# Tying the loads and the decoding of streamed weight tiles to places in the queues of a fused attention and MoE kernel

## The chip, the cores and the metric

The kernel runs on one core of a Trainium2 chip. The metric is the device time of one execution in microseconds (us); lower is better. Engines are called PE (TensorE), DVE (VectorE), ACT (ScalarE), POOL (GpSimd) and SP (SyncE, which issues DMAs here).

## What is computed

Attention with queries pooled in pairs, then two feed-forward layers. Inputs and weights are float64 on the host and reach the chip as pairs of 32-bit words.

```python
q_pool = q.reshape(B, H, S // 2, 2, D).mean(axis=3)          # B 2, H 8, S 1152, D 64
scores = np.matmul(q_pool, k.transpose(0, 1, 3, 2)) / np.sqrt(D)
attn = softmax(scores)                                        # max subtracted, 1e-9 in the sum
x = np.matmul(attn, v)                                        # -> [1152 tokens, 512]
h = x @ w_in                                                  # 512 -> 2048
g = (a0 + a1*h + a2*h**2 + a3*h**3) / (1 + |b0|*|h| + |b1|*h**2 + 1e-6)
x = g @ w_out                                                 # 2048 -> 512
h = x @ w2_in
g = np.maximum(h, 0) + np.log1p(np.exp(-np.abs(h)))
out = g @ w2_out
```

## The kernel before, in words

Every product is made from a high part and a low part of its operands (three matmuls for one). The attention works through NP = 8 pairs of heads. A pair has ST = 36 steps; step s makes one 128x288 block of scores (`s_step`, L436: two matmuls into a `pps` bank of PSUM, then the Exp on ACT, L449). Every second step `s_split` (L451) takes two blocks (tile `p`, 128x576): ACT casts them to the high part `ph` (L457) and POOL subtracts to get the low part `pl` (L121, a helper that all subtractions share). `pv` (L464, lines 471 to 473) multiplies both with V about seven steps later. While pair j runs its steps, the row maxima of pair j+1 are made (`p1_fill` on PE, L395; `p1_max` on DVE, L400), and its Q and K are turned and moved (`tr_k`, `tr_q`, `fcopy` DMAs at L209 on SP). There is no next pair during the last pair, so that DVE has little to do there.

The order is written out by hand: `at(t, fn)` collects functions with a step number on a common axis (pair j's steps are 36j to 36j+35), the list is sorted, and the functions run in that order. A tile scheduler then puts the instructions of every engine into a queue. It goes by that order but moves an instruction ahead of others as soon as its inputs and buffers are free in its own reckoning, and an engine works off its queue strictly in order. `behind(fn, engine)` keeps what `fn` issues on an engine behind a remembered instruction of that engine.

The 64 weight tiles (16 for each of four matrices) are streamed: `w_load` (L156) issues a 512 KB DMA on SP into one of two `wraw` buffers; `w_abs` (L171) makes the exponent right on ACT (L175) into one of three `pk` buffers; `w_conv` (L180) is two bit operations on DVE (L181 and L187; a third one, L184, only later); `w_split` (L191) casts the high part on ACT (L197) and subtracts the low part (L121, tile `w`) on POOL for the first NE = 3 tiles and on DVE for the rest. Together this is called decoding below. `pre` (L569) places the first 17 tiles in the attention: tiles 0 to 2 at steps 71, 107 and 143, and tiles 3 to 16 from step 242 on, one every four steps (load at t0, `w_abs` at t0+2, `w_conv` at t0+3 to t0+5, `w_split` at t0+7). The remaining tiles are decoded in the feed-forward part, paced by `w_step`. The tiles 3 to 16 live where the attention's buffers were: `close_early` at step 241, `close_even` at 262.

The first feed-forward layer works on 24 groups k of two column blocks: `up` (24 matmuls into a PSUM tile `h`, two buffers, L610), `act1_a` (three ACT passes over h), `act1_y` (three DVE passes; L636 is the last that reads h), `act1_b`, `act1_c`, and one group later `down1` (24 matmuls, `acc`, L660). The second layer does the same with a Softplus.

Of the kernel before, what the change touches and what calls it, by code (L numbers as in the profile page):

```python
# [21 lines left out]
    lv=0,  # L22
    pv=15,
    pvd=8,
    pq=8,
    tk=12,
    tkd=3,
# [21 lines left out]
    xb=19,  # L49
    w0=-1,  # L50
    wd=3,
    wc=25,
    wg=4,
    wh=1,
    ce=10,
# [30 lines left out]
def attn_moe_kernel(tc, q, k, v, w1_in, w1_out, moe_a, moe_b, w2_in, w2_out, out):  # L86
# [69 lines left out]
    def w_load(i):  # L156
        m, kind, f = order[i]
        src = (w1_in, w1_out, w2_in, w2_out)[2 * m + kind].bitcast(I32)
        raw = wst.tile([128, 512, 2], I32, tag="wraw", name="wraw", bufs=2)
        if kind == 0:  # L160
            nc.sync.dma_start(
                out=raw.rearrange("p (d f) e -> p d (f e)", d=ND),
                in_=src[:, f * 256:(f + 1) * 256].rearrange("(d p) f -> p d f", p=128),
            )
        else:
            nc.sync.dma_start(out=raw.rearrange("p f e -> p (f e)"), in_=src[f * 128:(f + 1) * 128, :])
        st["raw", i] = raw

    def w_abs(i):
        st["pk", i] = wst.tile([128, 512], I32, tag="pk", name="pk", bufs=3)  # L170
        o, hi = st["pk", i].bitcast(F32), st["raw", i][:, :, 1].bitcast(F32)  # L171
        if "second" in st:
            nc.scalar.activation(out=o, in_=hi, func=AF.Copy, scale=REBIAS)
        else:
            nc.scalar.activation(out=o, in_=hi, func=AF.Prelu, scale=REBIAS, alpha=SIGN)  # L175
            st["signed", i] = True
# [29 lines left out]
    QL = [[par[i].tile([74, 640], F32R, name=f"ql{i}{x}") for x in "ab"] for i in range(2)]  # L206
    V2 = [par[i].tile([128, 2, C, 192], F32R, name=f"v2{i}") for i in range(2)]
    def fcopy(out_, in_):
        nc.sync.dma_start(out=out_.bitcast(F32), in_=in_.bitcast(F32))  # L209

    def load_kq(j):
        b, h = j // NPB, 2 * (j % NPB)
# [225 lines left out]
    def s_step(j, s):  # L438
        g, c = divmod(s, C)
        x, half = divmod(g, 2)  # L440
        i = j % 2
        cs = qcols(x, half)
        ks = slice(c * 128, (c + 1) * 128)
        t = pps.tile([128, 512], F32, tag="s", name="s")[:, 0:HALF]
        nc.tensor.matmul(out=t, lhsT=KS[i][x][:, ks], rhs=QQ[i][x][:, cs], start=True, stop=False)  # L445
        nc.tensor.matmul(out=t, lhsT=KH[x][:, ks], rhs=QL[i][x][:, cs], start=False, stop=True)  # L446
        if s % 2 == 0:
            st["p"] = late.tile([128, 2, HALF], F32, tag="p", name="p", bufs=4)
        nc.scalar.activation(out=st["p"][:, s % 2], in_=t, func=AF.Exp)  # L449

    def s_split(j, s):  # L451
        p = st["pg", j, s]
        ph = late.tile([128, 2, HALF], F32R, tag="ph", name="ph", bufs=5)
        pl = late.tile([128, 2, HALF], F32R, tag="pl", name="pl", bufs=5)
        n = s // 2 + j * ST // 2
        if T["ph"] and n % T["ph"] == 0:
            nc.scalar.copy(out=ph, in_=p)  # L457
        else:
            nc.vector.tensor_copy(out=ph, in_=p)
        sub(nc.vector if T["lp"] and j == NP - 1 and n % T["lp"] == 0 else nc.gpsimd, pl, p, ph)  # L460
        for e in range(2):
            st["ph", j, s - 1 + e] = (ph[:, e], pl[:, e])
# [39 lines left out]
    for j in range(NP):  # L502
# [3 lines left out]
        for x in range(2):  # L506
            if j == 0:
                A(b1 + T["v0"] + T["pvd"] * x, lambda x=x: behind(lambda: prep_v(0, x), "act", "dve"), pr=7)
            else:
                if j == 1 and T["vb"]:  # L510
                    A(b1 + T["pv"] + T["pvd"] * x, lambda x=x: behind(lambda: prep_v(1, x), "act", "dves"), pr=7)
                else:
                    A(b1 + T["pv"] + T["pvd"] * x, prep_v, j, x, pr=7)
        if j == 0:
            A(b2 + 0, first_load)
            A(b2 + 1, warm, T["warm"])
# [49 lines left out]
            if g >= 2:  # L566
                A(b0 + C * g + T["xb"], xev_b, j, g, pr=3)

    def pre(i, t0, d, pool):  # L569
        at(t0, lambda: w_load(i))  # L570
        at(t0 + 2 * d, (lambda: behind(lambda: w_abs(i), "act")) if i < 2 else lambda: w_abs(i), 7)
        for n in range(3):
            at(t0 + 3 * d + d * n, lambda n=n: w_conv(i, n), 7)
        at(t0 + 7 * d, lambda: w_split(i, pool(), nc.vector if i >= NE else nc.gpsimd), 8)

    for i in range(NE):
        pre(i, ST * min(i + 2, NP - 2) + T["w0"] + 9 * max(0, i - NP + 4), T["wd"], lambda: we)

    def close_early():
        early.release()  # L580
# [7 lines left out]
    at(tc0, close_early)  # L588
    at(ST * (NP - 1) + T["ce"], close_even)
    for i in range(NRA + NRB):  # L590
        pre(NE + i, tc0 + 1 + T["wg"] * i, T["wh"], (lambda: st["wra"]) if i < NRA else (lambda: st["wrb"]))

    ph_ = pa_ = ap = wl_ = pt_ = pt2 = None

# [29 lines left out]

    def act1_a(h):
        m, s, p = T_("m", 2), T_("s", 2), T_("p", 2)
        nc.scalar.activation(out=m, in_=h, func=AF.Abs, scale=b_sb[:, 0:1])
        nc.scalar.activation(out=s, in_=h, func=AF.Square)
        nc.scalar.activation(out=p, in_=h, func=AF.Identity, scale=a_sb[:, 3:4], bias=a_sb[:, 2:3])
        return h, m, s, p  # L630

    def act1_y(h, m, s, p):
        V = nc.vector.scalar_tensor_tensor
        V(out=m, in0=s, scalar=b_sb[:, 1:2], in1=m, op0=ALU.mult, op1=ALU.add)
        nc.vector.tensor_mul(out=p, in0=h, in1=p)
        V(out=p, in0=p, scalar=a_sb[:, 1:2], in1=h, op0=ALU.add, op1=ALU.mult)  # L636
        return m, s, p

    def act1_b(m, r, p):
# [90 lines left out]
    if True:  # L730
# [66 lines left out]
        for k in range(NG + LAG1):  # L797
            if k == NG - 1:
                st["second"] = True
            if k < NG:  # L800
                for c, f in units[2 * k:2 * k + 2]:
# [2 lines left out]
                    h = up(0, c, f)  # L804
                    if c == (NCH - 1 if f < FH else 0):
                        freed.append(st["wp", (0, 0, f)])
                ga[k] = act1_a(h)
                ga[k] = act1_y(*ga[k])
            st["i"] = 2 * k
            w_pace()  # L810
            if 0 <= k - 1 < NG:
# [96 lines left out]
```

## Time and profile before

| | us |
|---|---|
| median of three runs | 764.52 (760.53, 764.52, 764.54) |
| the profiled execution | 760.95 |
| its span, first to last instruction | 759.2 |
| busy: PE / DVE / ACT / POOL | 725.5 / 540.8 / 493.7 / 295.0 |

The attention takes the first 338 us or so, the first layer goes to about 558 us, the second to the end. The page of the profile gives busy tenths in 40 slices of 19 us each. A busy PE is not a PE at its peak: matmuls overlap, so a stretch in which PE counts as busy throughout may still hold fewer matmuls than another.

### The profile page before, as it was taken

What the parts mean: (1) busy time and instruction counts of PE and PEld (TensorE: products, weight loads), DVE (VectorE), ACT (ScalarE), POOL (GpSimd) and SP (SyncE); (2) the same over time, 40 slices, a digit from 0 to 9 for tenths busy, and PEclk for the clock granted to TensorE, in tenths of its full rate; (3) what the DMA queues carried; (4) which work ended last, traced back from release to release, by engine and by line L of the source; (5) the groups of instructions that cost most, each with busy time, mean ns of one, the idle gap of its engine ahead of it and who ended that gap; (6) DMA issues with size and microseconds to landing.
All of it is one profiled execution on the core that took longest, in us unless ns stands there. A gap on an engine that the chain in (4) does not pass through costs nothing.

```text
span 759.2 us, 11696 instructions
## 1 busy us (share of the span) xinstructions
PE 725.5 (96%) x4273; PEld 680.3 (90%) x4273; DVE 540.8 (71%) x885; ACT 493.7 (65%) x921; POOL 295.0 (39%) x233
## 2 busy tenths in 40 slices
PE   8998999999999998887999999999999999999997
PEld 5698999999999997776999999999888789989986
DVE  5885877777777689389999999999997773111121
ACT  3377888888888888888777776876744553212120
POOL 5297888878787866960000000000243332000000
PEclk9999999999999999998999999999999999999999
DMA  6868664646454424023112221221234440001011
GB/s 184 203 155 177 166 163 103 138 105 149 100 119 101 93 64 130 30 83 111 56 57 60 80 84 56 83 60 52 84 111 139 137 141 0 1 1 42 0 42 43
DMA packets 60474, 70.32 MB, mean 93 GB/s; under 512 B 20008, under 2 KB 48512, under 8 KB 60416
## 3 DMA queue, kind: packets, MB, share of 16 engines
q1 hardware_dynamic: 59232, 68.58, 33.2%
q10 hardware_dynamic: 1184, 0.98, 0.4%
q8 instruction: 34, 0.56, 0.3%
q14 instruction: 24, 0.20, 0.1%
HBM read 47.71 MB, written 2.36 MB: 66 GB/s over the span
## 4 chain that ended last, share of the span: by engine, by line
PE 67%; DVE 17%; ACT 6%; DMA 6%; issue 3%; POOL 1%; SPq 0%; DVEq 0%; ACTq 0%; POOLq 0%
PE h L610 16%; PE p L395 10%; PE acc L702 9%; PE acc L660 8%; DMA wraw<-in_moe_w_in_dram 5%; PE s L445 4%; PE pv L473 4%; PE s L446 4%; PE pv L471 4%; PE pv L472 4%; DVE pk L187 3%; DVE pk L181 2%; DVE gl L121 2%; DVE w L121 1%; DVE pk L184 1%
## 5 line engine op out<-in xcount | busy, mean ns | idle before, releaser
L121 POOL TENSOR_TENSOR pl<-p,ph 128x576 fp32r<-128x576 f32 x144 | 208.6, 1465 | 60.4 <-ACT ph L457 33.8
L610 PE MATMUL h<-xh,w 128*128 128x384 f32 x768 | 198.6, 338 | 8.0 <-DVE p L636 8.0
L610 PEld LDWEIGHTS h<-xh,w 128*128 128x128 f32 x768 | 140.4, 190 | 11.0 <-issue 9.2
L400 DVE TENSOR_REDUCE nm<-p 128x1 f32<-128x384 f32 x216 | 116.5, 552 | 41.4 <-PE p L395 39.7
L121 POOL TENSOR_TENSOR w<-pk,w 128x512 fp32r<-128x512 f32 x26 | 41.5, 1598 | 250.0 <-ACT w L197 246.2
L449 ACT ACTIVATE p<-s 128x288 f32<-128x288 f32 x288 | 114.5, 408 | 25.4 <-PE s L446 23.2
L610 PE MATMUL h<-xl,w 128*128 128x384 f32 x384 | 129.7, 338 | 0.0
L121 DVE TENSOR_TENSOR gl<-p,gh 128x768 fp32r<-128x768 f32 (+1 forms) x49 | 48.4, 991 | 98.4 <-ACT gh L621 98.2
L457 ACT CAST ph<-p 128x576 fp32r<-128x576 f32 x144 | 96.9, 673 | 2.6
L660 PE MATMUL acc<-gh,w 128*128 128x384 f32 x384 | 92.7, 336 | 1.1 <-ACT gh L621 1.1
L473 PE MATMUL pv<-pl,v 128*128 128x288 f32 x288 | 87.0, 302 | 4.6 <-POOL pl L121 4.6
L702 PE MATMUL acc<-w,gh 128*128 128x512 f32 x288 | 90.3, 395 | 0.4 <-ACT gh L621 0.3
L471 PE MATMUL pv<-ph,v 128*128 128x288 f32 x288 | 86.2, 299 | 0.0
L472 PE MATMUL pv<-ph,v 128*64 128x288 f32 x288 | 85.1, 295 | 0.0
L690 ACT ACTIVATE p<-h 128x768 f32<-128x768 f32 (+1 forms) x25 | 19.5, 783 | 89.2 <-PE h L610 89.2
L610 PEld LDWEIGHTS h<-xl,w 128*128 128x128 f32 x384 | 72.7, 189 | 0.0
L660 PEld LDWEIGHTS acc<-gh,w 128*128 128x128 f32 x384 | 68.7, 188 | 2.1 <-ACT gh L621 2.1
L702 PEld LDWEIGHTS acc<-w,gh 128*128 128x128 f32 x288 | 53.5, 188 | 12.2 <-ACT gh L621 1.2
L473 PEld LDWEIGHTS pv<-pl,v 128*128 128x128 f32 x288 | 54.4, 189 | 8.3 <-POOL pl L121 7.0
L660 PE MATMUL acc<-gl,w 128*128 128x384 f32 x192 | 59.5, 338 | 1.0 <-DVE gl L121 1.0
L197 ACT CAST w<-pk 128x512 fp32r<-128x512 f32 x64 | 39.6, 619 | 31.8 <-DVE pk L187 31.8
L702 PE MATMUL acc<-w,gl 128*128 128x512 f32 x144 | 57.0, 396 | 1.1 <-DVE gl L121 1.1
(147 smaller groups left out, 1488.0 us busy)
## 6 DMA issues: line engine op xcount, KB each, us to landing
wraw<-in_moe_w_in_dram SPq DMA_DIRECT2D x32, 512.0 KB, 4.0
wraw<-in_moe_w_out_dram SPq DMA_DIRECT2D x32, 512.0 KB, 3.2
vr<-in_v_dram SPq DMA_DIRECT2D x8, 576.0 KB, 3.9
kr<-in_k_dram SPq DMA_DIRECT2D x15, 288.0 KB, 4.1
qr<-in_q_dram SPq DMA_DIRECT2D x15, 256.0 KB, 4.3
out_dram<-m SPq DMA_DIRECT2D x15, 128.0 KB, 1.8
kha<-ks0a SPq DMA_DIRECT2D x4, 288.0 KB, 3.1
khb<-ks0b SPq DMA_DIRECT2D x4, 288.0 KB, 4.3
```

Source lines behind the costliest of these rows:

```text
L121: return eng.tensor_tensor(out=o, in0=a, in1=b, op=ALU.subtract)
L197: nc.scalar.copy(out=w[:, 0], in_=g)
L395: m = nc.tensor.matmul(out=o, lhsT=l, rhs=r, start=(a == 0), stop=(a == len(mm) - 1))
L400: nc.vector.tensor_reduce(out=st["nm", j][:, t, e:e + 1], in_=st.pop(("p1", j, u)), axis=AX.X, op=ALU.max, negate=True)
L449: nc.scalar.activation(out=st["p"][:, s % 2], in_=t, func=AF.Exp)
L457: nc.scalar.copy(out=ph, in_=p)
L471: nc.tensor.matmul(out=st["pv", j, g], lhsT=h, rhs=ph, start=(c == 0), stop=False)
L472: nc.tensor.matmul(out=st["pv", j, g][0:64], lhsT=l, rhs=ph, start=False, stop=False)
L473: nc.tensor.matmul(out=st["pv", j, g], lhsT=h, rhs=pl, start=False, stop=(c == C - 1))
L610: nc.tensor.matmul(out=h, lhsT=w[:, wi, wd], rhs=x[:, d, xcols(c)], start=(n == 0), stop=(n == 3 * ND - 1))
L660: nc.tensor.matmul(out=st["acc", c, d], lhsT=w[:, wi, wd], rhs=g, start=(first and n == 0), stop=(last and n == 2))
L702: nc.tensor.matmul(out=st["acc", c, t], lhsT=g[:, t * 128:(t + 1) * 128], rhs=w[:, wi], start=(first and n == 0), stop=(last and n == 2))
```

## The change

- `pre` is rewritten: the load of a tile is placed at t0 and kept behind the last `fcopy` on SP, `w_abs` is placed at t0+5 and kept behind the last Exp on ACT, `w_conv` comes at t0+6 to t0+8, `w_split` at t0+10 and its ACT cast again behind the last Exp.
- Tiles 0 to 2 start at steps 72, 108 and 144. Tiles 3 to 16 start 11 steps earlier (`wc` 25 to 14: loads at steps 231, 235 and so on), which puts their `w_abs` 8 steps and their `w_split` 8 steps earlier; `close_early` moves with them to step 230, and the last pair's `prep_v` from steps 231 and 239 to 224 and 227.
- `wraw` gets three buffers, `pk` two.
- In the last pair every second cast to `ph` (nine of 18) is made by DVE.
- In the first layer `act1_a` makes `p` first, `act1_y` makes `m` last, and for the first two groups both are scheduled with high priority.

```diff
-    wc=25,
+    wc=14,
...
-        raw = wst.tile([128, 512, 2], I32, tag="wraw", name="wraw", bufs=2)
+        raw = wst.tile([128, 512, 2], I32, tag="wraw", name="wraw", bufs=3)
...
-        st["pk", i] = wst.tile([128, 512], I32, tag="pk", name="pk", bufs=3)
+        st["pk", i] = wst.tile([128, 512], I32, tag="pk", name="pk", bufs=2)
...
-        if T["ph"] and n % T["ph"] == 0:
+        if j == NP - 1 and n % 2:
+            nc.vector.tensor_copy(out=ph, in_=p)
+        else:
             nc.scalar.copy(out=ph, in_=p)
-        else:
-            nc.vector.tensor_copy(out=ph, in_=p)
...
-                    A(b1 + T["pv"] + T["pvd"] * x, prep_v, j, x, pr=7)
+                    A(b1 + (T["pv"] + T["pvd"] * x if j < NP - 1 else T["pe"] + T["ped"] * x), prep_v, j, x, pr=7)
...
-    def pre(i, t0, d, pool):
-        at(t0, lambda: w_load(i))
-        at(t0 + 2 * d, (lambda: behind(lambda: w_abs(i), "act")) if i < 2 else lambda: w_abs(i), 7)
+    def pre(i, t0, pool):
+        at(t0, lambda: behind(lambda: w_load(i), "sp"))
+        at(t0 + 5, lambda: behind(lambda: w_abs(i), "exp"), 7)
         for n in range(3):
-            at(t0 + 3 * d + d * n, lambda n=n: w_conv(i, n), 7)
-        at(t0 + 7 * d, lambda: w_split(i, pool(), nc.vector if i >= NE else nc.gpsimd), 8)
+            at(t0 + 6 + n, lambda n=n: w_conv(i, n), 7)
+        at(t0 + 10, lambda: behind(lambda: w_split(i, pool(), nc.vector if i >= NE else nc.gpsimd), "exp"), 8)
 
     for i in range(NE):
-        pre(i, ST * min(i + 2, NP - 2) + T["w0"] + 9 * max(0, i - NP + 4), T["wd"], lambda: we)
+        pre(i, ST * (i + 2), lambda: we)
...
     def act1_a(h):
         m, s, p = T_("m", 2), T_("s", 2), T_("p", 2)
+        nc.scalar.activation(out=p, in_=h, func=AF.Identity, scale=a_sb[:, 3:4], bias=a_sb[:, 2:3])
         nc.scalar.activation(out=m, in_=h, func=AF.Abs, scale=b_sb[:, 0:1])
         nc.scalar.activation(out=s, in_=h, func=AF.Square)
-        nc.scalar.activation(out=p, in_=h, func=AF.Identity, scale=a_sb[:, 3:4], bias=a_sb[:, 2:3])
...
-        V(out=m, in0=s, scalar=b_sb[:, 1:2], in1=m, op0=ALU.mult, op1=ALU.add)
         nc.vector.tensor_mul(out=p, in0=h, in1=p)
         V(out=p, in0=p, scalar=a_sb[:, 1:2], in1=h, op0=ALU.add, op1=ALU.mult)
+        V(out=m, in0=s, scalar=b_sb[:, 1:2], in1=m, op0=ALU.mult, op1=ALU.add)
...
-                ga[k] = act1_a(h)
-                ga[k] = act1_y(*ga[k])
+                with tc.high_priority() if k < 2 else ExitStack():
+                    ga[k] = act1_a(h)
+                    ga[k] = act1_y(*ga[k])
```

## Rows read from the trace of the kernel before

**Rows 1.** The page: busy tenths of PE in 40 slices
```profile
PE   8998999999999998887999999999999999999997
```
**Rows 2.** Windows: stretch, length, busy us (instructions) of PE, PEld, DVE, ACT, POOL; clock, DMA share, GB/s
```profile
33.90:76.30 42.40, 38.68 (x244) 36.30 (x244) 31.34 (x66) 31.98 (x71) 32.99 (x26) 0.96 0.74 175
76.30:114.40 38.10, 37.43 (x258) 36.22 (x258) 31.80 (x62) 33.38 (x75) 31.29 (x25) 1.00 0.62 162
114.40:151.10 36.70, 36.70 (x258) 36.21 (x258) 26.24 (x56) 31.43 (x72) 30.03 (x25) 1.00 0.53 123
...
261.10:301.40 40.30, 36.02 (x240) 34.21 (x239) 35.52 (x61) 34.57 (x78) 28.92 (x21) 1.00 0.36 100
...
301.40:332.00 30.60, 27.19 (x185) 24.09 (x183) 15.77 (x26) 28.01 (x67) 27.05 (x20) 1.00 0.17 52
...
346.90:358.10 11.20, 7.44 (x32) 7.47 (x33) 10.79 (x15) 9.77 (x15) 0.00 (x0) 0.70 0.36 114
...
400.00:500.00 100.00, 99.47 (x570) 98.61 (x569) 97.67 (x130) 75.10 (x104) 0.00 (x0) 1.00 0.23 74
```
**Rows 3.** Timeline of SP, ACT and PE, 52 to 61 us: start, length, what, idle before
```profile
52.66 0.60 SPq L161 DMA_DIRECT2D wraw<-in_moe_w_in_dram  x1
...
59.20 0.66 ACT L175 ACTIVATE pk<-wraw 128x512 f32<-128x512 f32 x1 [3.60 <-DMA wraw<-in_moe_w_in_dram]
...
60.78 0.40 PE L445 MATMUL s<-qq0b,ks0b 128*128 128x288 f32 x1 [2.85 <-ACT p L449]
```
**Rows 4.** Timeline of DVE in pair 1: a bit operation of an early decoded tile
```profile
82.45 1.46 DVE L187 SCALAR_TENSOR_TENSOR pk<-wraw,pk 128x512 int32<-128x512 int32 x1
```
**Rows 5.** Tile wraw, 0 to 300 us: time from issue to landing
```profile
DMA to landing us min/median/max: 4.1/5.9/6.7
```
**Rows 6.** Timelines of ACT and PE in pair 6: another wait for a load
```profile
285.69 0.67 ACT L175 ACTIVATE pk<-wraw 128x512 f32<-128x512 f32 x1 [2.69 <-DMA wraw<-in_moe_w_in_dram]
...
287.28 0.40 PE L445 MATMUL s<-qq0b,ks0b 128*128 128x288 f32 x1 [2.25 <-ACT p L449]
```
**Rows 7.** Timelines of POOL and DVE in the last pair
```profile
314.81 9.72 POOL L121 TENSOR_TENSOR pl<-p,ph 128x576 fp32r<-128x576 f32 x7
...
325.77 2.80 POOL L121 TENSOR_TENSOR pl<-p,ph 128x576 fp32r<-128x576 f32 x2 [1.24 <-PE s L446]
...
329.19 3.51 POOL L121 TENSOR_TENSOR pl<-p,ph 128x576 fp32r<-128x576 f32 x2 [0.61 <-ACT ph L457]
333.52 1.46 POOL L121 TENSOR_TENSOR pl<-p,ph 128x576 fp32r<-128x576 f32 x1 [0.82 <-ACT ph L457]
...
327.41 1.46 DVE L181 TENSOR_SCALAR pk<-pk 128x512 int32<-128x512 int32 x1 [0.79 <-ACT pk L175]
...
333.63 1.90 DVE L121 TENSOR_TENSOR w<-pk,w 128x512 fp32r<-128x512 f32 x1
```
**Rows 8.** Groups of instructions, 301.4 to 332 us: busy us, mean ns, idle before
```profile
L121 POOL TENSOR_TENSOR pl<-p,ph 128x576 fp32r<-128x576 f32 x18 | 26.2, 1479 | 3.0 <-PE s L446 1.2 <-ACT ph L457 1.2 <-POOL pl L121 0.4
...
L457 ACT CAST ph<-p 128x576 fp32r<-128x576 f32 x17 | 11.4, 673 | 0.0
...
L197 ACT CAST w<-pk 128x512 fp32r<-128x512 f32 x3 | 1.9, 625 | 0.0
...
L121 POOL TENSOR_TENSOR xl<-xs,xh 128x288 fp32r<-128x288 f32 x2 | 1.6, 806 | 1.1 <-ACT xh L494 1.1
```
**Rows 9.** Timelines of PE and DVE where the first layer begins
```profile
335.67 0.51 PE L610 MATMUL h<-xh,w 128*128 128x384 f32 x2
...
346.87 1.01 DVE L634 SCALAR_TENSOR_TENSOR m<-s,b_sb,m 128x768 f32<-128x768 f32 x1
...
350.66 0.98 PE L610 MATMUL h<-xh,w 128*128 128x384 f32 x2 [5.68 <-DVE p L636]
...
358.07 1.20 PE L660 MATMUL acc<-gh,w 128*128 128x384 f32 x6
```
**Rows 10.** Waits of PE from 400 us to the end: total us, times, longest
```profile
PE h L610 <- DVE p L636: 2.3, 2, 1.3
```

More of the change, by code (lines that the diff above doesn't have):

```diff
@@ L24 @@
     pvd=8,
+    pe=8,
+    ped=3,
     pq=8,
@@ L208, in fcopy @@
     def fcopy(out_, in_):
-        nc.sync.dma_start(out=out_.bitcast(F32), in_=in_.bitcast(F32))
+        st["last", "sp"] = nc.sync.dma_start(out=out_.bitcast(F32), in_=in_.bitcast(F32)).ins
     def load_kq(j):
@@ L448, in s_step @@
             st["p"] = late.tile([128, 2, HALF], F32, tag="p", name="p", bufs=4)
-        nc.scalar.activation(out=st["p"][:, s % 2], in_=t, func=AF.Exp)
+        st["last", "exp"] = nc.scalar.activation(out=st["p"][:, s % 2], in_=t, func=AF.Exp).ins
     def s_split(j, s):
@@ L590, in attn_moe_kernel @@
     for i in range(NRA + NRB):
-        pre(NE + i, tc0 + 1 + T["wg"] * i, T["wh"], (lambda: st["wra"]) if i < NRA else (lambda: st["wrb"]))
+        pre(NE + i, tc0 + 1 + T["wg"] * i, (lambda: st["wra"]) if i < NRA else (lambda: st["wrb"]))
     ph_ = pa_ = ap = wl_ = pt_ = pt2 = None
```

## The prediction

> **What bounds the kernel now.** I read the slices of PE first [rows 1]: PE is full nearly everywhere, and thinner in the first slice and the fourth, in the 16th to the 19th (285 to 361 us) and in the last. Saved work on another engine is worth something only in these places. The windows by pair of heads say how much [rows 2]. An undisturbed pair (114.40 to 151.10) takes 36.7 us with PE busy throughout. Pair 0 takes 42.4, pair 1 38.1 and pair 6 40.3. The last pair's 36 steps take only 30.6, since no maxima of a next pair are made; PE has 185 matmuls in them, where the 36.7 us of a full pair hold 258, so PE is not what sets this stretch. POOL is busy for 27.05 of the 30.6 us and ACT for 28.01.
>
> Then the single waits. At 52.66 SP issues a weight load; ACT already stands at the `w_abs` that needs it and waits 3.60 us, with the Exps queued behind it, and PE runs dry for 2.85 us [rows 3]. The clock falls after that: 0.96 on average over the 42.4 us of pair 0 [rows 2] is 3.4 us at the lower of the two levels (1.2 instead of 2.4 GHz), where half the work is done, so 1.7 us more. In pair 6 the same thing happens once: ACT waits 2.69 us for a load, PE 2.25 us for ACT [rows 6]. Where the first layer begins, PE starts `up` at 335.67 and reaches the first `down` only at 358.07, 22.4 us later [rows 9]; 5.68 us of it is one wait for DVE, whose first pass over h starts at 346.87 because late weight tiles are decoded ahead of it, and the clock is at 0.70 in the 11.2 us after that [rows 2, 9].
>
> **The change part by part**, in us of the profiled execution (760.95).
>
> *Loads kept on SP, tiles 0 to 2 moved out of the start.* The load that ran late belongs to tile 2; it and its decoding go to pair 4, those of tiles 0 and 1 to pairs 2 and 3. The wait of 2.85 and the 1.7 of clock go: 4.5. In pair 1 the early bit operations of tiles 3 and 4 go as well (one of them took 1.46 us [rows 4]), and pair 1 has 38.1 - 36.7 = 1.4 to give back. Together -5.9; the safe part is -4.5.
>
> *The price of that in pairs 2 to 4.* One tile more for each. The load stands on SP behind the copies of K, ahead of those of Q, none of which is needed at once; `w_abs` follows five steps later, 5 x 36.7/36 = 5.1 us, and loads in the attention landed after 4.1 to 6.7 us, 5.9 at the median [rows 5]. So ACT may stand still for up to 1.6 us, three times, and nearly all of such a wait reaches PE (2.25 of 2.69 [rows 6]): 0 to +4. The median would land 0.8 too late: 3 x 0.8 x 2.25/2.69 = 2.0. ACT comes to the `w_abs` itself a little after the step, so I take half, +1.
>
> *Pair 6.* Its excess is 40.3 - 36.7 = 3.6. Half of this is the wait for the load, which goes. The decoding of tiles 3 to 6 stays in its last 16 steps. I take -2 (-3.6 to 0).
>
> *The last pair.* This is the term that decides. Steps 252 to 287 get nine tiles' bit operations and nine `w_split`s, where three casts of weights stood [rows 8]. POOL and DVE get in each other's way there: undisturbed, seven `pl` take 9.72 us, 1.389 each, but with decoding beside them two take 3.51, and a bit operation lasts 1.46 and a subtraction 1.90 [rows 7], where the one at 314.81 ran alone. From 325.77 to 335.53 five `pl` and the DVE work of two tiles were done: 9.76 - 5 x 1.389 = 2.82, or 1.41 for a tile, as if only one of the two engines could work. Counted so, the last pair needs 18 x 1.389 = 25.0 and two `xl` 1.6 [rows 8] for POOL, 9 x 1.41 = 12.7 for the tiles, and the nine casts on DVE. No row shows such a cast on DVE; at least it costs nothing beside POOL, at most as much as on ACT, 0.67 [rows 8]; I take 0.38, half of 0.67 and a little, since a bit operation with one input ends 0.3 us after POOL lets go in [rows 7]: 3.4. The sum is 42.7 against 30.6: +12.1. ACT alone would be at 28.0 - 9 x 0.67 + 12 x 0.65 = 29.8 and is no bound, so the lower end is 0; the upper end is that of rival 2. That nothing of it can slip behind the attention follows from the code: `w_abs` is pinned to its step and needs a `pk` buffer, of which there are two, so a late subtraction holds up ACT and with it the Exps.
>
> Here the Trainium skill speaks against the change. SBUF — State Buffer, section "SBUF: two separate sides", says that VectorE (in a two-port mode, or with two SBUF inputs) and GpSimd hold their shared port pair as an exclusive lock for the whole instruction and the other blocks fully. The rows agree that only one of the two works at a time. By the rule, +12.1 for the last pair would be the least that is possible, the sum -3.3 or later, and rival 1 would fall away.
>
> *The start of the first layer.* All 17 tiles are then decoded. Three groups of 24 matmuls at the full clock are 12.5 (24 in 4.2, since 570 of them take 99.5 [rows 2]), the last `pv` some 1, and the first `down` waits a little for its input, which passes through nine passes of ACT and DVE: I estimate 15 for the 22.4, -7.5 (-9 to -5). DVE has been the bound there; its first pass moves from 11.2 us after the first `up` to some 6.5, so that -4.7 is the part that DVE confirms and the rest may be given back (rival 3).
>
> *The layers.* `up` waits 2.3 us for h to be freed [rows 10]; with `m` made last, h is free one pass earlier. Three `wraw` buffers let loads go earlier, while two `pk` buffers take freedom away. DVE is busy for 97.67 of 100 us there [rows 2], so no more than some 2 of each 100 can be gained: -1 (-3 to +1). The nine casts taken from ACT and the earlier `prep_v` of the last pair are hidden behind POOL and cost nothing more.
>
> Sum: -5.9 + 1 - 2 + 12.1 - 7.5 - 1 = -3.3.
>
> **The rivals.**
>
> 1. *The decoding fits into the last pair.* DVE is busy for only 15.77 of 30.6 us there, ACT would be no longer than now, and POOL has 3.5 us free; if the step that POOL sets is stretched only by a third of what I count (+4), the sum is -11.4: 752. For it: the first layer's gain is then whole. Against: five `pl` and two tiles took the full sum of both.
>
> 2. *DVE's own queue becomes the bound of the last pair (slower).* The two tiles of [rows 7] kept DVE from 327.41 to 335.53 without a pause: 4.06 each. Every four steps bring one such tile and one cast that may wait for a whole `pl` first, 0.38 + 1.39: 5.8 at most, where POOL and DVE in turn need 42.7/9 = 4.7. 9 x 5.8 = 52.2, +21.6 for the pair, and the sum is +6.2: 769.4. It decides as soon as DVE needs more than 4.7 us in four steps. Against: POOL makes only two `pl` in four steps and so can't hold DVE up for more than 2 x 1.389.
>
> 3. *Given back later (no change).* The start of the first layer is won for PE, but DVE, at 97.67%, sets its length: of -7.5 only -4.7 stays, and the loads of pairs 2 to 4 land late (+4, not +1) or the layers give nothing (0, not -1). The sum is between 0 and +3: 763 to 766. That the pins don't do what they say (a load still late on SP) ends here, too.
>
> **How the numbers follow.** The three runs before stand at 760.53, 764.52 and 764.54, the profiled one with the low one; I put the forecast on their mean, 763.2 - 3.3 = 759.9. Within 0.5% (3.8 us, about what a measurement of this kernel can tell from no change) of the median of 764.52 means 760.7 to 768.3. Forecast 0.42 (from 756 to 763, half of it beyond 0.5%), rival 1 0.26, rival 2 0.16, rival 3 0.16. Faster: 0.22 + 0.26 = 0.48; within: 0.20 + 0.13 = 0.33; slower: 0.16 + 0.03 = 0.19. The range takes in rival 1 at 752 with some 4 below it for the better ends of the single terms, and ends at rival 2: 748 to 770.
>
> **What would show it.** Pair 0 near 38 us and pair 1 near 36.7, with no wait of ACT for `wraw` before 110 us; pairs 2 to 4 still below 38. Pair 6 near 38. The last pair at 40 us or more with `pl` and DVE's operations taking turns: if it stays near 33 the sum is wrong by 9 us to the good, if it nears 50 to the bad. From the first `up` to the first `down` some 15 us, at the full clock. If PE's idle time from 400 us on grows, the gain was given back to DVE.

## The result, and the profile after

The changed kernel takes 772.25 us (771.3 to 773.07), the kernel before 764.53 (760.53 to 765.61): a ratio of 1.011, 95% interval 1.0072 to 1.0148. The change makes it slower by 1.1%; 759.9 was forecast, and 772.25 lies above the range. The profiled execution after takes 772.27 with a span of 770.3, 11.1 us more than that of the profiled one before, which was one of the low ones. The stages below compare these two.

The page of the changed kernel, busy tenths of PE and its granted clock in 40 slices of 19.3 us:

```profile
PE   7999999999999998778999999999899799999998
...
PEclk9999999999999998889999999999999999999999
```

The hole of the fourth slice [rows 1] is gone. The hole around the last pair is still there, the clock now drops in it, and a new hole stands in the 32nd slice (597 to 616 us), in the second layer.

I cut the span at instructions that every kernel here has: the first score matmul of each pair, the first `up`, the first `down` of either layer and the last `down`. Windows of the changed kernel between them, with the columns of [rows 2]: pairs 0, 1, 2, 6 and the last pair's 36 steps, then first `up` to first `down`, the first layer and the second:

```profile
33.53:70.62 37.09, 36.83 (x243) 34.87 (x243) 26.66 (x59) 30.06 (x67) 27.68 (x23) 1.00 0.69 160
70.62:107.31 36.69, 36.69 (x258) 36.19 (x257) 27.27 (x56) 31.45 (x72) 30.04 (x25) 1.00 0.54 124
107.31:145.95 38.64, 37.37 (x258) 36.37 (x257) 27.09 (x58) 32.40 (x74) 31.73 (x26) 1.00 0.57 130
...
258.95:293.47 34.52, 34.52 (x240) 34.09 (x239) 26.24 (x52) 31.07 (x69) 27.09 (x20) 1.00 0.46 125
293.47:337.47 44.00, 35.26 (x182) 29.78 (x181) 42.62 (x54) 30.75 (x72) 29.90 (x20) 0.84 0.37 115
342.61:364.90 22.29, 19.75 (x97) 19.01 (x96) 19.61 (x27) 14.44 (x21) 3.08 (x3) 0.85 0.26 80
364.90:563.58 198.68, 194.86 (x1112) 194.19 (x1112) 195.32 (x257) 149.47 (x204) 7.54 (x5) 0.99 0.22 70
563.58:766.80 203.22, 196.78 (x961) 173.95 (x960) 76.32 (x99) 61.91 (x93) 30.48 (x19) 0.98 0.16 52
```

The two layers of the kernel before, in the same view:

```profile
358.07:559.64 201.57, 197.07 (x1122) 194.22 (x1122) 197.13 (x259) 147.09 (x204) 9.13 (x4) 1.00 0.21 69
559.64:754.64 195.00, 193.46 (x961) 172.21 (x960) 73.34 (x98) 62.13 (x94) 28.05 (x19) 1.00 0.18 57
```

| us | before | after | forecast | came |
|---|---|---|---|---|
| to the end of pair 1 | 114.35 | 107.31 | -5.9 | -7.0 |
| pairs 2 to 4 | 110.11 | 115.02 | +1 | +4.9 |
| pair 6 | 40.34 | 34.52 | -2 | -5.8 |
| last pair, 36 steps | 30.22 | 44.00 | +12.1 | +13.8 |
| its end to the first `up` | 4.01 | 5.14 | 0 | +1.1 |
| first `up` to first `down` | 22.40 | 22.29 | -7.5 | -0.1 |
| first and second layer | 396.57 | 401.90 | -1 | +5.3 |

The rows add up to +12.2 where -3.3 was forecast; the span grew by 11.1, since the time behind the last `down` gives 1.0 back. The miss of some 15 us is the start of the first layer (7.4), the layers (6.3), pairs 2 to 4 (3.9) and the last pair with its end (2.8), less pair 6 (3.8) and the beginning (1.1).

**The last pair.** Groups of instructions of the changed kernel from 293.47 to 342.61 us (busy, mean ns, idle before): DVE's three steps of decoding and its casts, POOL's `pl`, ACT's `w_abs`:

```profile
L189 DVE SCALAR_TENSOR_TENSOR pk<-wraw,pk 128x512 int32<-128x512 int32 x10 | 13.2, 1324 | 0.2
L123 DVE TENSOR_TENSOR w<-pk,w 128x512 fp32r<-128x512 f32 x10 | 12.4, 1236 | 0.0
L183 DVE TENSOR_SCALAR pk<-pk 128x512 int32<-128x512 int32 x10 | 9.2, 921 | 1.2 <-ACT pk L177 1.1
L459 DVE CAST ph<-p 128x576 fp32r<-128x576 f32 x9 | 6.5, 723 | 0.0
...
L123 POOL TENSOR_TENSOR pl<-p,ph 128x576 fp32r<-128x576 f32 x21 | 33.7, 1612 | 15.7 <-DVE ph L459 9.2 <-issue 4.2 <-ACT ph L461 0.9
...
L177 ACT ACTIVATE pk<-wraw 128x512 f32<-128x512 f32 x10 | 6.7, 673 | 9.8 <-DVE w L123 9.7
```

DVE is busy for 42.62 of the 44.00 us, but with stretched instructions: the operation of line 189 takes 0.69 us where POOL is idle (at 350.22), and has a mean of 1.324 here. POOL waits 9.2 us for casts that stand in DVE's queue, and ACT 9.7 us for a `pk` buffer that DVE's subtraction hasn't freed. Timelines of DVE and POOL there (start, length):

```profile
302.46 0.41 DVE L183 TENSOR_SCALAR pk<-pk 128x512 int32<-128x512 int32 x1
302.91 1.79 DVE L189 SCALAR_TENSOR_TENSOR pk<-wraw,pk 128x512 int32<-128x512 int32 x1
304.62 1.90 DVE L123 TENSOR_TENSOR w<-pk,w 128x512 fp32r<-128x512 f32 x1
306.44 0.45 DVE L459 CAST ph<-p 128x576 fp32r<-128x576 f32 x1
...
302.62 3.35 POOL L123 TENSOR_TENSOR pl<-p,ph 128x576 fp32r<-128x576 f32 x2 [0.40 <-DVE ph L459]
306.97 1.42 POOL L123 TENSOR_TENSOR pl<-p,ph 128x576 fp32r<-128x576 f32 x1 [1.00 <-DVE ph L459]
```

Two `pl`, two operations of a tile, the cast, and round again: the two engines take turns, as in [rows 7]. DVE is the one whose queue has no room left (42.62 of 44.00 us); POOL stands idle for 14.1 of them.

**The start of the first layer.** Timelines of PE, ACT and DVE of the changed kernel:

```profile
342.62 0.39 PE L612 MATMUL h<-xh,w 128*128 128x384 f32 x1
...
356.16 0.75 PE L612 MATMUL h<-xh,w 128*128 128x384 f32 x2 [2.54 <-DVE p L637]
...
364.91 1.38 PE L662 MATMUL acc<-gh,w 128*128 128x384 f32 x7
...
350.22 0.44 ACT L496 CAST xh<-xs 128x288 fp32r<-128x288 f32 x1 [1.12 <-DVE xs L489]
350.69 0.99 ACT L629 ACTIVATE p<-h,a_sb 128x768 f32<-128x768 f32 x1
351.58 0.89 ACT L630 ACTIVATE m<-h,b_sb 128x768 f32<-128x768 f32 x1
352.36 0.81 ACT L631 ACTIVATE s<-h 128x768 f32<-128x768 f32 x1
...
353.20 0.96 DVE L636 TENSOR_TENSOR p<-h,p 128x768 f32<-128x768 f32 x1 [2.29 <-ACT s L631]
354.08 1.01 DVE L638 SCALAR_TENSOR_TENSOR m<-s,b_sb,m 128x768 f32<-128x768 f32 x1
355.00 1.01 DVE L637 SCALAR_TENSOR_TENSOR p<-p,a_sb,h 128x768 f32<-128x768 f32 x1
```

DVE is free from 350.91, 8.3 us after the first `up`, since the last two of the 17 tiles are still decoded behind it (their subtractions stand at 344.77 and 347.71) and the next tile's bit operations follow. Even so its first pass over h starts only 10.6 us after the first `up`, where 6.5 was forecast. It needs only h and `p`, ready at 351.68, but starts when ACT's third pass ends; in none of the 24 groups does it start earlier. And `m` is queued ahead of the second pass to `p` in 21 of 24, against the order in the code.

In the kernel before, DVE's first instruction of the evaluation, at 346.87, was `m` and not a pass over h [rows 9]. It needs ACT's `s`:

```profile
345.65 0.81 ACT L628 ACTIVATE s<-h 128x768 f32<-128x768 f32 x1
```

This ended at 346.46, so that the decoding ahead of it on DVE held `m` up by no more than 0.4 us.

**The second layer.** ACT's waits of the changed kernel from 560 to 650 us (total, times, longest), and one wait of PE in its timeline:

```profile
ACT pk L175 <- POOL w L123: 24.8, 18, 2.0
...
602.25 1.22 PE L704 MATMUL acc<-w,gh 128*128 128x512 f32 x2 [3.61 <-ACT gh L623]
```

The kernel before waits in the same place once:

```profile
ACT pk L173 <- POOL w L121: 1.9, 1, 1.9
```

### The profile page after: what moved, and what is told of

Same layout as the page of the kernel before. It is cut to its first block, busy times and chain, and to the rows that moved or that the text cites. A ratio compares the mean times of both kernels' runs of the same rounds, so it can differ in the third digit from the quotient of the medians.

```text
span 770.3 us, 11766 instructions
## 1 busy us (share of the span) xinstructions
PE 734.8 (95%) x4273; PEld 688.9 (89%) x4273; DVE 552.7 (72%) x894; ACT 491.2 (64%) x912; POOL 296.1 (38%) x233
## 5 line engine op out<-in xcount | busy, mean ns | idle before, releaser
L612 PE MATMUL h<-xh,w 128*128 128x384 f32 x768 | 199.5, 340 | 6.4 <-DVE p L637 6.4
L123 POOL TENSOR_TENSOR w<-pk,w 128x512 fp32r<-128x512 f32 x26 | 41.9, 1611 | 254.8 <-ACT w L199 253.4
L704 PE MATMUL acc<-w,gh 128*128 128x512 f32 x288 | 92.3, 402 | 4.8 <-ACT gh L623 4.6
L475 PE MATMUL pv<-pl,v 128*128 128x288 f32 x288 | 89.0, 309 | 8.1 <-POOL pl L123 7.9
L461 ACT CAST ph<-p 128x576 fp32r<-128x576 f32 x135 | 90.7, 672 | 2.6
L662 PE MATMUL acc<-gh,w 128*128 128x384 f32 x384 | 90.4, 335 | 0.0
L473 PE MATMUL pv<-ph,v 128*128 128x288 f32 x288 | 88.2, 306 | 0.8 <-ACT ph L461 0.4
L189 DVE SCALAR_TENSOR_TENSOR pk<-wraw,pk 128x512 int32<-128x512 int32 x64 | 63.1, 986 | 0.9
L473 PEld LDWEIGHTS pv<-ph,v 128*128 128x128 f32 x288 | 56.5, 196 | 2.1 <-ACT ph L461 1.4
```

The lines of the kernel that those rows point to most:

```text
L123: return eng.tensor_tensor(out=o, in0=a, in1=b, op=ALU.subtract)
L189: nc.vector.scalar_tensor_tensor(out=g, in0=raw[:, :, 0], scalar=29, in1=g, op0=ALU.logical_shift_right, op1=ALU.bitwise_or)
L473: nc.tensor.matmul(out=st["pv", j, g], lhsT=h, rhs=ph, start=(c == 0), stop=False)
L475: nc.tensor.matmul(out=st["pv", j, g], lhsT=h, rhs=pl, start=False, stop=(c == C - 1))
L612: nc.tensor.matmul(out=h, lhsT=w[:, wi, wd], rhs=x[:, d, xcols(c)], start=(n == 0), stop=(n == 3 * ND - 1))
L662: nc.tensor.matmul(out=st["acc", c, d], lhsT=w[:, wi, wd], rhs=g, start=(first and n == 0), stop=(last and n == 2))
```

## The experiments

Stages by the same cuts, in us of each profiled execution (p2-4: pairs 2 to 4; p7: 36 steps of the last pair; start: first `up` to first `down`; L1, L2: the layers):

| kernel | p2-4 | p6 | p7 | start | L1 | L2 | ratio to before, 95% |
|---|---|---|---|---|---|---|---|
| before | 110.1 | 40.3 | 30.2 | 22.4 | 201.6 | 195.0 | |
| after | 115.0 | 34.5 | 44.0 | 22.3 | 198.7 | 203.2 | 1.0072 to 1.0148 |
| e1 | 114.3 | 34.5 | 43.0 | 25.8 | 197.3 | 199.0 | 1.0037 to 1.0077 |
| e2 | 114.2 | 34.5 | 39.9 | 20.9 | 196.9 | 204.5 | 1.0043 to 1.0091 |
| e3 | 115.5 | 34.1 | 44.6 | 27.0 | 198.1 | 202.2 | 1.0142 to 1.0206 |
| e4 | 118.2 | 41.9 | 30.2 | 21.9 | 201.7 | 195.1 | 0.9978 to 1.0015 |
| e5 | 113.9 | 34.5 | 35.7 | 22.4 | 198.4 | 204.0 | 0.9964 to 1.0009 |
| e6 | 113.5 | 34.5 | 43.4 | 23.2 | 199.0 | 201.4 | 1.0056 to 1.0111 |
| e7 | 122.9 | 34.5 | 43.4 | 22.2 | 199.0 | 201.4 | 1.0215 to 1.0284 |
| e8 | 110.2 | 40.5 | 28.1 | 23.5 | 200.9 | 194.9 | 0.9932 to 0.9975 |
| e9 | 110.1 | 40.5 | 29.5 | 22.8 | 199.5 | 194.1 | 0.9955 to 1.0014 |
| e10 | 116.1 | 41.5 | 33.9 | 21.9 | 198.1 | 202.1 | 1.0070 to 1.0119 |
| e11 | 113.5 | 34.5 | 35.7 | 24.3 | 198.0 | 197.5 | 0.9899 to 0.9946 |
| e12 | 113.5 | 34.5 | 35.7 | 22.7 | 201.8 | 194.7 | 0.9884 to 0.9934 |
| e13 | 113.5 | 34.5 | 35.7 | 25.2 | 198.2 | 197.3 | 0.9904 to 0.9957 |
| e14 | 113.5 | 34.5 | 35.7 | 22.6 | 201.8 | 194.8 | 0.9860 to 0.9926 |
| e15 | 113.5 | 34.5 | 35.7 | 19.3 | 201.7 | 194.7 | 0.9834 to 0.9909 |

### e1: the buffers as before

```diff
-        raw = wst.tile([128, 512, 2], I32, tag="wraw", name="wraw", bufs=3)
+        raw = wst.tile([128, 512, 2], I32, tag="wraw", name="wraw", bufs=2)
...
-        st["pk", i] = wst.tile([128, 512], I32, tag="pk", name="pk", bufs=2)
+        st["pk", i] = wst.tile([128, 512], I32, tag="pk", name="pk", bufs=3)
```

> The changed kernel with the two buffer counts put back (wraw 2, pk 3). Theory A: the second layer lost 8 us (203.2 instead of 195.0 us from its first to its last down matmul) because w_abs waits for a pk buffer that POOL's subtraction still holds (ACT waited 24.1 us on it there); with three buffers the second layer goes back to about 195, and the 10.4 us that ACT waited for DVE's subtraction in the last pair go, but the pair itself stays at 43 us or more for its 36 steps, since POOL and DVE exclude each other. Sum about -8, near the kernel before. Rival B: the two pk buffers are also what stretched the last pair; then that falls to 36 us as well, and the kernel is some 8 us faster than before. Rival C: the buffers do nothing: 772.

The second layer gets back 4.3 of its 8.2 us, the last pair 1.0. ACT's wait for a `pk` that POOL holds is gone in the second layer; both counts went back at once, so that the 4.3 us is put down to `pk` by this wait, not by a run with `pk` alone. The start is 3.5 longer than in the changed kernel; what sets it is e12's to e15's question.

### e2 and e5: the last pair's casts, then its subtractions

e2 leaves all casts to ACT; e5 does this and gives the last pair's 18 `pl` to DVE.

```diff
-        if j == NP - 1 and n % 2:
+        if False:
             nc.vector.tensor_copy(out=ph, in_=p)
...
-    lp=0,
+    lp=1,          (e5 alone)
```

> The changed kernel with all 18 casts of the last pair on ACT again. If POOL and DVE exclude each other (theory A), nine casts cost the pair about 9 x 0.4 to 0.5 = 3.5 to 4.5 us of shared time, and its 36 steps go from 44.5 to about 41, for ACT has room (35 of 49 us busy). If instead the tie of pl to DVE's queue is the trouble (POOL waited 9.2 us for ph from DVE), up to 9 us go. If the casts were a relief to ACT, the pair gets longer by 9 x 0.57 = 5 us.

> The changed kernel with all casts of the last pair on ACT (as in e2_casts_on_act) and with the last pair's 18 subtractions pl on DVE instead of POOL. Theory A (POOL and DVE exclude each other): with POOL out of the last pair DVE's operations fall back to their undisturbed lengths (0.4, 0.7, 0.7 for a tile, some 0.7 for a pl), DVE needs 18 x 0.65 + 9 x 1.55 + 5.5 = 31 us, ACT some 34, so that the 36 steps go from 39.9 (e2) to 33 to 36 us although DVE now does all the work. Rival B (DVE has simply too many instructions in the last pair): 12 us more on DVE, the pair goes to 45 us or more.

Windows of the last pair's 36 steps in e2 and in e5 (columns as in [rows 2]):

```profile
292.55:332.43 39.88, 32.22 (x182) 26.82 (x181) 35.16 (x46) 34.71 (x80) 31.11 (x21) 0.91 0.39 129
```

```profile
293.55:329.21 35.66, 30.67 (x180) 24.07 (x178) 34.19 (x62) 34.01 (x80) 6.00 (x5) 1.00 0.45 142
```

The nine casts cost 4.1 us (3.4 counted). Then the test that decides: e5 takes the `pl` from POOL, so that DVE does the work of both, and the stretch is shorter by another 4.2. DVE is busy for 34.19 us with 62 instructions, where 46 took 35.16 in e2. Groups of instructions of DVE in these stretches, e2 and then e5, say why:

```profile
L123 DVE TENSOR_TENSOR w<-pk,w 128x512 fp32r<-128x512 f32 x9 | 11.5, 1280 | 0.0
```

```profile
L123 DVE TENSOR_TENSOR pl<-p,ph 128x576 fp32r<-128x576 f32 x16 | 11.7, 749 | 0.1
...
L123 DVE TENSOR_TENSOR w<-pk,w 128x512 fp32r<-128x512 f32 x9 | 6.1, 682 | 0.4 <-ACT w L199 0.4
```

With POOL out of the way a subtraction of `w` takes 0.682 us, not 1.280, and a `pl` on DVE takes 0.749, where POOL took 1.389 [rows 7]. So it was the turns of POOL and DVE that set the last pair. In e5 ACT (34.01) and DVE (34.19) are both busy for nearly all of it. The clock stays at 1.00 in e5, where the changed kernel had 0.84 with PE thin.

### e3 and e10: the place of the late tiles, and the ties

e3 shifts the 14 late tiles back by 11 steps (`wc` 14 to 25) and leaves the ties. e10 leaves the places and unties the late tiles' load, `w_abs` and `w_split`.

```diff
+    def tied(i, fn, engine):
+        behind(fn, engine) if i < NE else fn()
...
-        at(t0, lambda: behind(lambda: w_load(i), "sp"))
+        at(t0, lambda: tied(i, lambda: w_load(i), "sp"))
...            (w_abs and w_split likewise)
```

> The changed kernel with the 14 late tiles placed 11 steps later again (wc 25), all else as changed. Theory A (decoding beside POOL costs its full DVE time wherever it stands): three tiles' decoding leave the attention, 3 x 1.41 = 4.2 us off the pair, and the start of the first layer gets them back as DVE work of about the same size; together within 3 us of the changed kernel. Rival B (the early placement is what lengthened the last pair): the pair goes back to some 36 us and the kernel gains 6 us or more.

> The changed kernel, with the loads and the first decoding steps of the late weight tiles not tied to a place any more; their casts and the rest as in the change. If the ties crowd the last pair: its 36 steps fall from 44.0 to between 30 and 38 us, and the span by 6 to 14 us. If it is the number of tiles and casts on DVE and POOL at the same time: the 36 steps stay at 42 to 45 us and the span within 2 us of 770.

e3: the last pair stays at 44.6, and the start grows to 27.0, as neither theory had it. Shifting changes which nine tiles fall into these 36 steps, not that one comes every four steps; I had not seen that. e10: neither theory as written. The last pair falls by 10.1, but pair 6 grows by 6.9 and pair 4 by 2.2, and the span of 768.0 is within 2.3 of the changed kernel's. Freed of the ties the tiles move out of the last pair and cost nearly as much where they go: the ties decide the place of the loss, the work on DVE beside POOL its size.

### e4, e6, e7: tiles 0 to 2

e4 is the kernel before with only tiles 0 to 2 placed and tied as in the change; e6 is the changed kernel with their loads 8 steps earlier, e7 with all their steps 13 earlier.

```diff
-        at(t0, lambda: behind(lambda: w_load(i), "sp"))
+        at(t0 - (8 if i < NE else 0), lambda: behind(lambda: w_load(i), "sp"))     (e6)
...
-        pre(i, ST * (i + 2), lambda: we)
+        pre(i, ST * (i + 2) - 13, lambda: we)                                      (e7)
```

> The kernel before with only the first three weight tiles placed as in the change (loads behind SP's last copy, w_abs and w_split behind an Exp, pairs 2 to 4); all other tiles as before. Theory A: pair 0 falls from 42.4 to 37.1 and pair 1 may, as in the changed kernel, but pairs 2 to 4 take 38.0 to 38.6 instead of 36.7: together about -2 us. Rival B: the late tiles, which the scheduler used to pull into pair 1, come even earlier or crowd pair 1, and the gain is lost: 0 or slower.

> The changed kernel with only the loads of tiles 0 to 2 issued 8 steps earlier; their decoding stands where it stood. Theory A (w_abs waits for a load that lands late, 2.3 us in pairs 2 to 4 together): pairs 2 to 4 lose most of their excess of 1.3 to 1.9 us each, down to 37.2 or less. Rival B (ACT is too full at steps 5 to 12 of a pair for two more passes, whenever the data land): they stay at 38 to 38.6.

> The changed kernel with tiles 0 to 2 placed 13 steps earlier as a whole (load at step 23 of the pair before, w_abs at 28, w_split at 33), where the pairs make no turns of K and Q and ACT waits for PE now and then. Rival B of e6_loads_earlier expects pairs 1 to 4 at 36.7 to 37.2; its theory A expects little change, since the load has the same five steps and lands as late.

e4 has pairs 0 and 1 at 37.1 and 36.7: the first gain belongs to this part alone. It brings nothing (0.9978 to 1.0015), since pairs 2 to 4 give back 8.1, 5.0 of it in pair 4, where tile 2 meets bit operations of late tiles that the scheduler has pulled forward. Waits from 107 to 222 us in the changed kernel, and the same wait in e6:

```profile
PE tk L328 <- ACT p L451: 3.4, 3, 1.2
...
ACT pk L177 <- DMA wraw<-in_moe_w_in_dram: 2.3, 3, 1.1
```

```profile
PE tk L328 <- ACT p L451: 2.7, 3, 0.9
```

With the loads 8 steps earlier ACT's wait for them is gone, and pairs 2 to 4 are only 1.5 shorter (115.0 to 113.5) of the 4.9 lost: 37.8 each, between the two theories. What is left looks like ACT: at these steps the tile's two instructions come on top of its other work, and the turns of K on PE wait for ACT, which they never do there in the kernel before. No run shows this by itself; e7, which moves the two to other steps, meets another loss and is worse: each of the pairs 1, 2 and 3 takes 4 us more than in the changed kernel. The row of it is in the last section.

### e8 and e9: one part alone on the kernel before

e8 is the kernel before with the last pair's `pl` on DVE (`lp` 0 to 1), e9 the kernel before with only the new order of `act1_a` and `act1_y` and the high priority.

> The kernel before with only the last pair's subtractions pl on DVE. The last pair is bound by POOL there (27 of 30.6 us busy, seven pl back to back), so theory A expects 36 steps at the pace of ACT, some 28 to 30 us, and with no POOL beside it the late decoding that follows is undisturbed: the start of the first layer some 2 us earlier. Together -2 to -5 us. If DVE gets too full, the pair is longer than 30.2.

> The kernel before with only the new order of ACT's evaluation in the layers (act1_a, act1_y and the high priority of the first two groups). Theory A (the layers' gain belongs to this part and is given back in the second layer): attention unchanged, first up to first down 21.5 to 23, first layer 198 to 199 (before: 201.6), second layer 198 to 199 (before: 195.0), span within 1.5 us of before. Theory B (the gain stays and the change's loss in the second layer is its two pk buffers alone): first layer 198 to 199, second layer 195, span 2.5 to 4 us shorter. Theory C (the gain of the first layer comes from the weight tiles' places): first layer 201 to 202, span as before.

e8 is faster by 0.5% (0.9953), 2.1 us of it in the last pair. e9: 0.9985, no change that can be told; its profiled execution has both layers together shorter by 3.0, the start longer by 0.4. Theories A and C fall by the layers' lengths, but the times don't bear out B's 2.5 to 4 us either.

### e11 and e12: what the single runs add up to, and the order of the evaluation

e11 is the changed kernel with e1's buffers, e5's casts and subtractions and e6's loads. e12 is e11 with the evaluation's order as before.

> The changed kernel with all attention casts on ACT, the last pair's POOL subtractions on DVE, the loads of tiles 0 to 2 eight steps earlier, and two raw buffers and three pk buffers as before. If the causes add up as read singly: pairs 2 to 4 at 37.8 each, the last pair's 36 steps 35.7 (changed kernel 44.0), both layers together 396 to 397 (changed kernel 401.9), span 753 to 756, 0.5 to 0.8% faster than before. If the slack is taken up later (the first layer's tiles are late when the last pair is shorter): last pair 35.7, but first up to first down or the layers longer by 3 to 6, span 757 to 761, as before.

> The combined kernel of the last experiment with the order of the layers' evaluation (act1_a, act1_y, no high priority) as before the change. In the changed kernel DVE's first pass over h starts after ACT's third pass over h in all 24 groups; before, its first pass was m, which doesn't read h and began while ACT's third pass ran. Theory A (the new order takes this overlap away and brings nothing): DVE's first pass 0.5 to 1 us sooner after the first up, first up to first down 23 to 24 (combined 24.3), the layers as in the combined kernel or up to 2 shorter, span 752 to 754. Theory B (the new order is worth the 2.1 us that the first layer showed with it alone): first layer 199 to 200 (combined 198.0), span 755.5 to 757.

e11 takes 757.3 us, 0.9923 of before. The single causes add up: pairs 2 to 4 at 37.8 each, the last pair 35.7, both layers 395.4. Against e8 alone (0.9932 to 0.9975) the rest of the change has thus gained about 0.3%, within the intervals. e12 shows the order for what it is: with the old one, and without the high priority, which goes back with it, the first layer is 3.8 longer, the second 2.8 shorter, the start 1.7 shorter. The whole, 756.56 against 757.3, is within the intervals. Windows of the two layers in e11 and in e12:

```profile
355.12:553.10 197.98, 194.53 (x1112) 192.68 (x1112) 193.58 (x255) 147.23 (x201) 7.01 (x4) 1.00 0.22 70
553.10:750.56 197.46, 193.62 (x961) 172.20 (x960) 75.87 (x99) 62.59 (x95) 28.65 (x19) 1.00 0.17 57
```

```profile
353.61:555.37 201.76, 197.50 (x1120) 195.54 (x1119) 196.87 (x259) 147.15 (x204) 7.20 (x4) 0.99 0.21 69
555.37:750.06 194.69, 193.07 (x961) 172.33 (x960) 72.80 (x97) 61.57 (x92) 28.06 (x19) 1.00 0.17 57
```

DVE has four instructions and 3.3 us less in the first layer of e11, and two and 3.1 us more in the second (the other two stand in the start): work that has crossed the cuts, not work saved.

### e13, e14, e15: the start of the first layer

e13 is e11 with the cast `xh` of the attention's last evaluation on DVE, so that ACT needn't wait for `xs` ahead of its first pass over h; e14 is e12 with the same edit; e15 is e14 with the next weight tile's `w_abs` kept behind the three passes of ACT over the first h.

```diff
-        nc.scalar.copy(out=xh[o], in_=xs)
+        if j == NP - 1 and g == 3:
+            nc.vector.tensor_copy(out=xh[o], in_=xs)
+        else:
+            nc.scalar.copy(out=xh[o], in_=xs)
...            (e15, in w_step; "g0" is ACT's third pass over the first h)
-                w_abs(cnt["abs"])
+                if ("last", "g0") in st and cnt["abs"] == n0 + 1:
+                    behind(lambda: w_abs(cnt["abs"]), "g0")
+                else:
+                    w_abs(cnt["abs"])
```

> The combined kernel with the cast xh of the attention's last evaluation made by DVE, so that ACT doesn't stand still for DVE's xs ahead of its first pass over h. In the combined kernel the first h is complete at 337.2 and ACT begins with it at 340.08; PE then waits 4.21 us for DVE. Theory A (ACT's queue sets the start of the first layer): ACT's first pass 2 to 3 us sooner after the first up, PE's wait 1.5 to 3, first up to first down 20 to 22.5 (combined 24.3), span 750 to 752. Theory B (DVE's decoding sets it): ACT sooner, DVE's first pass within 0.7 us of where it was, span 753.5 to 755.

> Both edits on the combined kernel: the old order of the evaluation and the last cast xh on DVE. If ACT's queue sets the start of the first layer and the new order brings nothing: first up to first down 19.5 to 22, span 749 to 751.5. If the new order is worth 2 us in the layers: span 752 to 754. If DVE's decoding sets the start: 23.5 to 25 and a span of 753 to 756.

> The kernel of e14, with the w_abs of the tile whose load lands late (ACT stood 3.32 us for it at 340.47, ahead of its first pass over h) kept behind the third pass over the first h. Theory A (ACT's in-order queue sets the start of the first layer, one waiting instruction after the other): ACT begins with the first h within 1.5 us of the end of its matmuls, DVE's first pass 9 us or less after the first up, first up to first down 19 to 21 (e14: 22.6), span 750.5 to 752.5. Theory B (DVE and the rate of decoding set it): first up to first down 22 to 23.5 or the first layer 1 to 3 longer, span 753 to 755.5.

e13 gains nothing: in ACT's timeline the wait for `xs` is gone, and the next instruction of the queue waits instead, for a load, ahead of the same pass:

```profile
341.28 0.67 ACT L177 ACTIVATE pk<-wraw 128x512 f32<-128x512 f32 x1 [3.33 <-DMA wraw<-in_moe_w_in_dram]
341.98 0.99 ACT L632 ACTIVATE p<-h,a_sb 128x768 f32<-128x768 f32 x1
```

e14 has the same wait, 3.32 us (22.6). e15 takes it out of the way. Its timelines of ACT, DVE and PE, and its window from first `up` to first `down`:

```profile
337.80 0.91 ACT L632 ACTIVATE m<-h,b_sb 128x768 f32<-128x768 f32 x1 [0.58 <-PE h L615]
...
339.82 1.01 DVE L640 SCALAR_TENSOR_TENSOR m<-s,b_sb,m 128x768 f32<-128x768 f32 x1
...
343.10 0.59 PE L615 MATMUL h<-xh,w 128*128 128x384 f32 x2 [1.17 <-DVE p L642]
```

```profile
330.91:350.20 19.29, 16.65 (x94) 15.34 (x93) 18.16 (x28) 16.11 (x25) 2.39 (x2) 1.00 0.34 107
```

ACT now waits for PE's h, not h for ACT; DVE starts 8.9 us after the first `up`; PE's longest wait is 1.17, where it was 2.54 in the changed kernel and 4.21 in e11, and the granted clock is 1.00 throughout, where it was 0.85 in the changed kernel and 0.92 in e14. The start takes 19.3 and the whole kernel 752.74 us (751.85 to 754.32), 0.9872 of before: 1.3% faster than the kernel before, 2.4% faster than the changed one by the two ratios.

## Why the prediction was wrong

**The beginning (-5.9, came -7.0): right.** The early wait, the clock and pair 1's excess all went, and e4 shows that this part alone does it.

**Pairs 2 to 4 (+1, came +4.9): a cost looked for in the wrong place.** I priced only the late landing, 0 to +4; e6 puts that at 1.5. ACT's own two instructions per tile, which stand among the Exps and casts that PE waits for, were counted at nothing. That they are the other 3.4 us is read from PE's waits and not shown by a run.

**Pair 6 (-2, came -5.8): the measure was wrong.** I took 36.7 as its undisturbed length, from a pair with 258 matmuls; [rows 2] show 240 for pair 6, and 34.52 is what these take. The excess was 5.8, and all of it went.

**The last pair (+12.1, came +13.8): right in mechanism and nearly in size.** The price of 1.41 for a tile, read from one stretch of [rows 7], and DVE and POOL in turn gave 42.7; 44.0 came (30.2 before by the cuts used here, 30.6 in the prediction). Without the casts the same sum is 39.3, and e2 took 39.9. That the price came out so well has some luck in it: the 9.76 us it is taken from hold waits of POOL for ACT too [rows 7]. The casts were 4.1, not 3.4; the buffers add 1.0 (e1). Rival 1 is out. Rival 2, whose time of 769.4 lies nearest, has the right engine: DVE's queue is the full one. Its size is wrong: 42.62 us over nine tiles are 4.7 for each four steps, not 5.8, and its 52.2 us for the pair didn't come. The Trainium skill's SBUF — State Buffer, section "SBUF: two separate sides", has VectorE (in a two-port mode, or with two SBUF inputs) and GpSimd hold a shared port pair as an exclusive lock; e5 agrees, where DVE alone needed 35.7 us for what it and POOL did in 39.9.

**The start of the first layer (-7.5, came -0.1): the step that failed.** I read in [rows 9] that decoding on DVE was ahead of its first pass, took it away, and asked only whether DVE would then be the next bound. The reading was wrong already: what starts at 346.87 is `m`, which had to wait for ACT's `s` until 346.46, and the first pass over h was the next instruction of DVE. I didn't look at the engines that feed DVE. Of the 10.6 us that came in place of 6.5, 6.8 pass until PE has h complete (349.46), 1.2 until ACT begins with it (350.69), and 2.5 until ACT's third pass ends (353.17). The rest of the miss, 3.2 us, comes behind that, where the granted clock averages 0.80 (356.16 to 364.91). Rival 3 falls with the same step: at the start there was no gain to give back.

First, the first `up` is no clean beginning. I counted 4.2 us for h. `pv` of the last pair are mixed into the first 24 `up`, so that it took 5.1 before, at a granted clock of 1.00. The changed kernel needs 6.8 for the same 33 matmuls: PE was busy for only 2.63 of the 5.15 us ahead of them, and the granted clock averages 0.75 in them, a mix of the two levels.

Second, ACT's in-order queue. In the changed kernel it holds a `w_abs`, which waits for DVE's subtraction (0.75 us), and the last evaluation's cast, which waits for DVE too (1.12 us), ahead of the first pass over h. With the other parts put right this queue is the longer delay: in e11 ACT begins with h 2.9 us after it is complete, behind the cast, and in e14, which has the cast elsewhere, 3.5 us, behind a `w_abs` that waits for its load. e15 takes both out of the way and gets 3.3 of the 22.6 us; e13 and e14, which take only the cast, get nothing.

Third, "p first" brings nothing. DVE's pass never starts ahead of the end of ACT's third pass in the 24 groups, whereas before the change DVE's first instruction was `m`, which doesn't read h and ran beside ACT's third pass (346.87 [rows 9], ACT ending at 347.34). e12 puts this, with the high priority, at 1.7 us at the start. Why the pass waits so the trace doesn't say. The Trainium skill, PSUM — Partial Sum Buffer, section "PSUM bank collisions raise a hardware error", states that the compiler's scheduler adds a dependency between instructions of different engines that touch the same bank and partitions of PSUM, reads too. The 24 starts agree with that.

Even e15's 19.3 is far from the 15 that I forecast: DVE is busy for 18.16 of them, with the last tiles' decoding still among its work. So "all 17 tiles are then decoded" didn't hold either, and what is left is mostly DVE's.

**The layers (-1, came +5.3): a sentence without a number.** "Two `pk` buffers take freedom away" was written and then given a range of -3 to +1. In the second layer POOL makes the subtraction, about 1.6 us each, and a buffer is free only after it; with two, `w_abs` stands in ACT's queue for the last but one subtraction 18 times, 24.8 us in 90, with the casts `gh` behind it that PE needs. e1 prices this at 4.3. The first layer's -2.9 goes with DVE work that went over into the second (e11 against e12).

With the start alone put right the sum is -3.3 + 7.4 = +4.1, and with the `pk` buffers +8.4: the start is enough for the wrong sign.

## What to carry to other kernels

When a wait is taken away, write down the next instruction in the same queue and what it waits for; then do so for the queue of the engine that feeds the one that was waiting. Price a buffer that is taken away by its longest user: who holds it, for how long, and what stands in order behind the instruction that needs the next one. Two engines that have to take turns aren't two engines: where DVE and POOL share a stretch, giving everything to the quicker one can beat sharing it (e5, e8).

## What the runs showed of the hardware that I had not expected

A DVE instruction can be held for several POOL instructions in a row, not for one. Timelines of e7, POOL and DVE (start, length):

```profile
100.82 5.56 POOL L123 TENSOR_TENSOR pl<-p,ph 128x576 fp32r<-128x576 f32 x4
...
101.38 5.28 DVE L183 TENSOR_SCALAR pk<-pk 128x512 int32<-128x512 int32 x1 [0.23 <-ACT pk L177]
```

The bit operation that takes 0.41 us at 302.46 in the changed kernel lasts 5.28 here, until 0.28 us after the end of four `pl` that followed each other without a gap. The same happens three times, once for each of the tiles 0 to 2 (5.27 to 5.30 us), and each time PE waits 3.4 us for DVE's next results. e7 is 2.5% slower than the kernel before, 1.4% slower than the changed one by the two ratios. So in these three places the price of a shared stretch wasn't bounded by one instruction of the other engine: four `pl` in a row went first.
